# Rolling VectorE, ScalarE and the q projection of a one-token attention kernel, with wo loaded in five pieces

## The chip, the cores and the metric

The kernel runs on one core of a Trainium2 chip. The metric is the device time of one execution in microseconds (us). All runs that are compared here are in the fast state. Each kernel of the experiments was timed in five rounds beside the kernel before on the same chip; the experiments ran on three chips, on which the kernel before had medians of 662.74 (twice) and 662.91 us.

## The reference

One decode step of an attention block and a small feed-forward block, added up. Only the cache is large: K and V are 32 x 4 MB each.

```python
B, D, H, Sk, Dh, Dff = 2, 512, 32, 8192, 128, 1792      # one new token for each of 2 rows
xn = layernorm(x)
q = (xn @ wq) per head                                   # wq is 4 MB
p = softmax(q . k_cache * Dh**-0.5)                      # for each of the 64 (row, head) pairs
o = p . v_cache                                          # then o @ wo, wo is 4 MB
out = x + o @ wo + relu(xn @ w1) @ w2                    # w1, w2: 1792 KB each
```

## The kernel before: the parts that matter here

Two heads are one "pair", 4 MB of K and 4 MB of V. There are 32 pairs, two buffers for K and two for V. SyncE issues all large loads from one queue; wq borrows the second V buffer.

```python
nc.sync.dma_start(vs[1][:], wq).then_inc(dV[1], 16)
...
load_k(0); load_k(1); load_v(0)                  # SyncE
for t in range(NP - 1):
    if t + R < NP:
        sp.wait_ge(pT, NG * (t + 1))             # K buffer free: all transposes of pair t done
        load_k(t + R)
    sp.wait_ge(sW, t + 1)                        # V buffer free: weighted sum of pair t-1 done
    load_v(t + 1)
... x8, w1, w2, then wo in 3 pieces: cuts = (0, 16, 28, WJ) ...
```

TensorE projects q with 128 small matmuls written out one by one, and only then enters its loop over pairs:

```python
pe.wait_ge(dV[1], 16)                            # wq has landed
for h in range(H):
    for kt in range(KT):
        i = pe.matmul(qp[:, h, :], lhsT=wq_sb[:, kt, h*Dh:(h+1)*Dh], rhs=xnT[:, kt, :], ...)
i.then_inc(sQ, 1)
...
with pe.Fori(16, 16 * (NP // R) + 1, 16) as n16: # already rolled: two pairs a round
    for r in range(R):
        pe.reg_add(reg, reg, 1)
        step(r, reg, n16)                        # transposes of K, scores, weighted sum of the pair before
```

VectorE and ScalarE are written out over all 32 pairs in the kernel before (`for t in range(NP)`): they copy the transposed K from PSUM, find the maximum and do the exponential.

## Time and profile before

| | kernel before |
|---|---|
| time, median of 3 | 662.87 us (662.78 to 663.01) |
| span in the profile | 660.4 us |
| moved by DMA | 280.5 MB of data, mean 425 GB/s |
| TensorE, VectorE, ScalarE busy | 83%, 38%, 36% |
| q projection | 13.30 to 16.85 us |
| K0's transposes start / K2 issued | 24.27 / 36.53 us |
| last byte of wo / end of TensorE's wo matmuls | 655.75 / 656.82 us |

The page's lines for this kernel stand in the prediction below. A digit in the forty slices is a busy share in tenths. A row of stretches gives, from left to right, the stretch, its length, the busy time of TensorE's matmuls, its weight loads, VectorE, ScalarE and GpSimd with their counts, the granted clock, the DMA share and GB/s. The one thing to see is that the DMA engines are full from 3 us to 652 us (a DMA share of 0.99 to 1.00 in each stretch between), so the engines' busy shares decide nothing by themselves.

The 16 DMA engines can also be told apart. The records of packets carry no engine number, but from 60 to 600 us 16 packets are open in 95.6% of the time, and a 4 MB transfer is 128 packets of 32 KB, eight for each of 16. Strung together where one ends and the next starts, the packets give 16 chains, in which 98% of the gaps are under 30 ns. That a chain is an engine is an inference, and two chains that run in step can be taken for each other. How many engines still move data at a given time can be counted without chains, from the packets that are open then, and the groups below agree with that count.

### The profile page before, as it was taken

How to read it: one execution, taken by the hardware profiler on the slowest of the kernel's cores; microseconds unless marked ns; L12 is line 12 of the kernel's file. 1: busy time of each engine (PE TensorE's matmuls, PEld its weight loads, DVE VectorE, ACT ScalarE, POOL GpSimd, SP SyncE). 2: the span in 40 equal slices, each digit the busy share in tenths (PEclk: the TensorE clock that was granted, in tenths of full speed). 3: DMA queues.
4: the chain of work that ended last, by engine and by line, in shares of the span. 5: the costliest groups of instructions: out<-in, count | busy, mean ns of one | idle time of the engine just before them, and what ended most of it. 6: DMA issues, size and time to landing. Idle time of an engine off the chain costs nothing.

```text
span 660.4 us, 26876 instructions
## 1 busy us (share of the span) xinstructions
PE 551.0 (83%) x12864; PEld 537.0 (81%) x12864; DVE 251.4 (38%) x433; ACT 236.7 (36%) x389; POOL 8.5 (1%) x44
## 2 busy tenths in 40 slices
PE   2577999898887889788798987887997878987976
PEld 2577999888887889788798887887987878987875
DVE  1233544344343434434344443343443433443411
ACT  1242444343433334333243343333343333343410
POOL 1000000000000000000000000000000000000000
PEclk9999999998898999889899898899898989997985
DMA  9999999999999999999999999999999999999995
GB/s 381 416 438 429 424 439 427 437 427 431 437 429 437 427 431 433 429 437 429 431 435 427 439 429 431 435 427 439 427 431 433 429 439 425 435 433 429 437 417 246
DMA packets 10133, 280.73 MB, mean 425 GB/s; under 512 B 1154, under 2 KB 1156, under 8 KB 1284
## 3 DMA queue, kind: packets, MB, share of 16 engines
q1 hardware_dynamic: 10112, 280.50, 98.9%
q8 instruction: 10, 0.16, 0.1%
q14 instruction: 7, 0.06, 0.0%
q10 hardware_dynamic: 4, 0.00, 0.0%
HBM read 280.50 MB, written 0.00 MB: 425 GB/s over the span
## 4 chain that ended last, share of the span: by engine, by line
DMA 62%; PE 34%; ACT 1%; issue 1%; SPq 0%; DVE 0%
DMA ks<-in_A_k_cache_dram 56%; PE tp L233 21%; PE Sc L240 10%; DMA wo_sb<-in_A_wo_dram 5%; PE ot L253 3%; ACT kT L380 1%; PE ot L356 0%; PE Sc L288 0%; PE Sc L291 0%; SPq L171 0%; SPq L168 0%; SPq L166 0%; SPq L149 0%; SPq L167 0%; SPq L147 0%
## 5 line engine op out<-in xcount | busy, mean ns | idle before, releaser
L233 PE MATMUL tp<-identb,ks 128*128 128x128 bf16 x4096 | 324.9, 229 | 77.8 <-DMA ks<-in_A_k_cache_dram 75.9
L380 DVE COPY kT<-tp 128x1024 bf16<-128x1024 bf16 x320 | 219.7, 691 | 332.9 <-PE tp L233 332.7
L233 PEld LDWEIGHTS tp<-identb,ks 128*128 128x128 bf16 x4096 | 256.1, 103 | 81.3 <-DMA ks<-in_A_k_cache_dram 79.1
L380 ACT COPY kT<-tp 128x1024 bf16<-128x1024 bf16 x192 | 194.3, 1012 | 249.6 <-PE tp L233 249.6
L240 PE MATMUL Sc<-q,kT 128*128 128x64 bf16 x4096 | 216.3, 196 | 3.4 <-ACT kT L380 3.4
L240 PEld LDWEIGHTS Sc<-q,kT 128*128 128x128 bf16 x4096 | 178.4, 100 | 6.7 <-ACT kT L380 6.7
L253 PE MATMUL ot<-prm,vs 128*128 128x64 bf16 x4224 | 157.6, 193 | 8.5 <-issue 5.0
L253 PEld LDWEIGHTS ot<-prm,vs 128*128 128x128 bf16 x4224 | 140.5, 98 | 11.4 <-issue 8.8
L483 ACT COPY nm<-Sc 128x2 f32<-128x2 f32 x32 | 5.1, 160 | 118.2 <-PE Sc L291 118.2
L487 ACT ACTIVATE prm<-Sc,nm 64x128 bf16<-64x128 f32 x64 | 25.8, 402 | 1.4
L425 DVE TENSOR_REDUCE mcol<-Sc 64x1 bf16<-64x128 f32 x64 | 18.6, 291 | 17.6 <-PE Sc L240 17.2
L473 ACT COPY OTf<-ot 128x2 f32<-128x2 f32 x33 | 5.3, 160 | 35.3 <-PE ot L253 35.3
L430 DVE TENSOR_REDUCE mx<-Sc 1x2 bf16<-1x128 bf16 x32 | 8.9, 279 | 16.9 <-PE Sc L288 16.9
L203 POOL COPY q<-qb 128x2 bf16<-128x2 bf16 x32 | 5.8, 184 | 582.3 <-PE Sc L240 568.6
L487 ACT ACTIVATION_READ_ACCUMULATOR prm<-Sc,nm 64x1 f32 x64 | 11.8, 185 | 0.0
L218 PE MATMUL ot<-xnT,vs 128*128 128x2 bf16 x128 | 3.6, 165 | 8.3 <-DMA vs<-in_A_wq_dram 8.3
L218 PEld LDWEIGHTS ot<-xnT,vs 128*128 128x128 bf16 x128 | 3.5, 104 | 8.4 <-issue 8.4
L288 PE MATMUL Sc<-identb,mcol 128*1 128x128 bf16 x32 | 7.0, 217 | 0.0
L356 PE MATMUL ot<-OX,wo_sb 128*128 128x2 bf16 x128 | 3.7, 166 | 3.1 <-DMA wo_sb<-in_A_wo_dram 3.1
L356 PEld LDWEIGHTS ot<-OX,wo_sb 128*128 128x128 bf16 x128 | 3.6, 104 | 3.3 <-DMA wo_sb<-in_A_wo_dram 1.9
L291 PE MATMUL Sc<-mx,onesb 1*128 1x2 bf16 x32 | 5.5, 172 | 0.0
L436 DVE CAST xT<-tp 128x8 f32<-128x8 bf16 x1 | 0.2, 166 | 12.5 <-PE Sc L327 12.5
(49 smaller groups left out, 29.4 us busy)
## 6 DMA issues: line engine op xcount, KB each, us to landing
ks<-in_A_k_cache_dram SPq DMA_DIRECT2D x32, 4096.0 KB, 26.8
vs<-in_A_v_cache_dram SPq DMA_DIRECT2D x32, 4096.0 KB, 31.6
vs<-in_A_wq_dram SPq DMA_DIRECT2D x1, 4096.0 KB, 12.2
w_sb<-in_B_w_dram SPq DMA_DIRECT2D x2, 1792.0 KB, 25.9
wo_sb<-in_A_wo_dram SPq DMA_DIRECT2D x1, 2048.0 KB, 32.3
wo_sb<-in_A_wo_dram SPq DMA_DIRECT2D x1, 1536.0 KB, 35.5
wo_sb<-in_A_wo_dram SPq DMA_DIRECT2D x1, 512.0 KB, 36.3
xsb<-in_A_x_dram ACTq DMA_DIRECT2D x1, 2.0 KB
```

Source lines behind the costliest of these rows:

```text
L203: g.tensor_copy(q2[t % R][:], qb[:, 2 * t:2 * t + 2]).then_inc(sQ1, 1)
L218: i = pe.matmul(qp[:, h, :], lhsT=wq_sb[:, kt, h * Dh:(h + 1) * Dh], rhs=xnT[:, kt, :], start=(kt == 0), stop=(kt == KT - 1),)
L233: t = pe.transpose(tp[e % 4][:, i, :], ks[r][:, kk * Dh:(kk + 1) * Dh], identb[:])
L240: t = pe.matmul(Sc[r][:, 2 * kk:2 * kk + 2 * REP], lhsT=kT[e % 4][:, i, :], rhs=rep(q2[r][:]), start=True, stop=True,)
L253: t = pe.matmul(ot[r][:, 0:2 * REP], lhsT=vs[r][:, kk * Dh:(kk + 1) * Dh], rhs=rep(prm[r][:, kk, :]), start=(kk == 0), stop=(kk == KB - 1),)
L288: pe.transpose(tr_of(r), mcol[r][:], identb[:]).then_inc(sT, 1)
L291: pe.matmul(bc_of(r), lhsT=onesb[:], rhs=mx[r][:], start=True, stop=True).then_inc(sB, 1)
L356: t = pe.matmul(fin[:, c, :], lhsT=w[:, j, c * P:(c + 1) * P], rhs=act[:, j, :], start=(first and j == j0 and c == 0), stop=(last and j == ...
L380: fn(kT[e % 4][:], tp[e % 4][:]).then_inc(kR[e], 1)
L425: m = v.tensor_reduce(out=mcol[i][half, :], in_=S_of(i)[half, :, u], axis=AX.X, op=ALU.max)
L430: v.tensor_reduce(out=mx[i][:], in_=tr_of(i).rearrange("o (u m) -> o u m", u=2), axis=AX.X, op=ALU.max, negate=True,).then_inc(sX, 1)
L487: x = a.activation(out=prm[i][half, :, u], in_=S_of(i)[half, :, u], func=ACTF.Exp, bias=nm[i][half, u:u + 1], scale=1.0, accum_out=RS[half ...
```

## The change

The intent is less code and fewer instruction fetches: VectorE and ScalarE get loops as TensorE has one, the q projection becomes eight rounds of 16 matmuls, the engines' programs stand directly in the critical section, and wo comes in five pieces, so that fewer matmuls follow the last landing.

```diff
-    cuts = (0, 16, 28, WJ)
+    cuts = (0, 16, 22, 27, 30, WJ)
...
-    block = nc.Block(no_gpsimd_drain=True)
-    block.__enter__()
-    @block.sync
+    @(lambda f: f(nc.sync))                       # the same for the other four engines
...
-        for h in range(H):
-            for kt in range(KT):
-                i = pe.matmul(
-                    qp[:, h, :],
-                    lhsT=wq_sb[:, kt, h * Dh:(h + 1) * Dh],
+        HL = 4
+        with pe.Fori(0, H // HL) as hg:
+            for h in range(HL):
+                for kt in range(KT):
+                    i = pe.matmul(
+                        ot[1][:, bass.ds(hg * (HL * Bsz) + h * Bsz, Bsz)],
+                        lhsT=vs[1][:, bass.ds(hg * (HL * Dh) + (kt * H + h) * Dh, Dh)],
...
-        for t in range(NP):                       # VectorE; the same for ScalarE
-            i = t % R
+        def pair(i, n):
...
+        with v.Fori(0, NP // R):
+            for r in range(R):
+                v.reg_add(reg, reg, 1)
+                pair(r, reg)                      # waits count up to a register
```

(The semaphore of the transposes is split into one per group, so that the rolled engines can wait for a register's value; the diff is cut.)

More of the change, by code (lines that the diff above doesn't have):

```diff
@@ L121 @@
     dV = [sem(f"dV{i}") for i in range(R)]
-    dW = [sem(f"dW{i}") for i in range(5)]
+    dW = [sem(f"dW{i}") for i in range(2 + 5)]
     sG, sI, sQ, sQ1 = sem("sG"), sem("sI"), sem("sQ"), sem("sQ1")
     sV, sA, sE = sem("sV"), sem("sA"), sem("sE")
-    pT, sS, sT, sB, sW = sem("pT"), sem("sS"), sem("sT"), sem("sB"), sem("sW")
+    sS, sT, sB, sW = sem("sS"), sem("sT"), sem("sB"), sem("sW")
+    pT = [sem(f"pT{e}") for e in range(NG)]
     kR = [sem(f"kR{e}") for e in range(NG)]
-    sM, sX, sP, sO = sem("sM"), sem("sX"), sem("sP"), sem("sO")
+    sM, sX, sP, sO, sN = sem("sM"), sem("sX"), sem("sP"), sem("sO"), sem("sN")
     sH, sF = sem("sH"), sem("sF")
@@ L133 @@
     wo_v = A_wo.rearrange("(p j) n -> p j n", j=WJ)
-    cuts = (0, 16, 28, WJ)
+    cuts = (0, 16, 22, 27, 30, WJ)
+    NC = len(cuts) - 1
     qp = ot[1][:, 0:N].rearrange("p (h b) -> p h b", b=Bsz)
@@ L161, in _ @@
             if t + R < NP:
-                sp.wait_ge(pT, NG * (t + 1))
+                sp.wait_ge(pT[NG - 1], t + 1)
                 load_k(t + R)
@@ L168, in _ @@
         sp.dma_start(w2_sb[:], B_w2.rearrange("(p j) n -> p j n", j=FT)).then_inc(dW[1], 16)
-        for c in range(3):
+        for c in range(NC):
             sl = slice(cuts[c], cuts[c + 1])
@@ L175, in _ @@
         ).then_inc(dO, 16)
-    @block.gpsimd
+    @(lambda f: f(nc.gpsimd))
     def _(g):
@@ L203, in _ @@
             g.tensor_copy(q2[t % R][:], qb[:, 2 * t:2 * t + 2]).then_inc(sQ1, 1)
-    @block.tensor
+    @(lambda f: f(nc.tensor))
     def _(pe):
@@ L214, in _ @@
         pe.wait_ge(dV[1], 16)
-        wq_sb = vs[1][:].rearrange("p (kt n) -> p kt n", kt=KT)
-        for h in range(H):
-            for kt in range(KT):
-                i = pe.matmul(
-                    qp[:, h, :],
-                    lhsT=wq_sb[:, kt, h * Dh:(h + 1) * Dh],
-                    rhs=xnT[:, kt, :],
-                    start=(kt == 0),
-                    stop=(kt == KT - 1),
-                )
-        i.then_inc(sQ, 1)
+        HL = 4
[5 more added lines that the diff above has]
+                        lhsT=vs[1][:, bass.ds(hg * (HL * Dh) + (kt * H + h) * Dh, Dh)],
+                        rhs=xnT[:, kt, :],
+                        start=(kt == 0),
+                        stop=(kt == KT - 1),
+                    )
+            i.then_inc(sQ, 1)
         def rep(ap):
@@ L233, in transposes @@
                 t = pe.transpose(tp[e % 4][:, i, :], ks[r][:, kk * Dh:(kk + 1) * Dh], identb[:])
-            t.then_inc(pT, 1)
+            t.then_inc(pT[e], 1)
         def scores(r, e, n):
@@ L368, in _ @@
         pe.wait_ge(sV, 104)
-        for c in range(3):
+        for c in range(NC):
             pe.wait_ge(dW[2 + c], 16)
-            t = project(wo_sb, OX, cuts[c], cuts[c + 1], last=(c == 2))
+            t = project(wo_sb, OX, cuts[c], cuts[c + 1], last=(c == NC - 1))
         t.then_inc(sH, 1)
@@ L380, in kcopy @@
         fn(kT[e % 4][:], tp[e % 4][:]).then_inc(kR[e], 1)
-    @block.vector
+    @(lambda f: f(nc.vector))
     def _(v):
@@ L405, in _ @@
         v.tensor_copy(xnT[:], tpx).then_inc(sV, 1)
-        v.wait_ge(sQ, 2)
+        v.wait_ge(sQ, 1 + H // 4)
         v.tensor_scalar(
@@ L414, in _ @@
         ).then_inc(sV, 94)
-        for t in range(NP):
-            i = t % R
+        def pair(i, n):
             for e in range(NG):
                 if e not in ON_ACT:
-                    v.wait_ge(pT, NG * t + e + 1)
+                    v.wait_ge(pT[e], n)
                     kcopy(v, e)
-            v.wait_ge(sS, t + 1)
+            v.wait_ge(sS, n)
             for u in range(2):
@@ L428, in _ @@
             m.then_inc(sM, 1)
-            v.wait_ge(sT, t + 1)
+            v.wait_ge(sT, n)
             v.tensor_reduce(
@@ L433, in _ @@
             ).then_inc(sX, 1)
+        reg = nc.alloc_register(mybir.EngineType.DVE, "pairno_v")
+        v.reg_mov(reg, 0)
+        with v.Fori(0, NP // R):
+            for r in range(R):
+                v.reg_add(reg, reg, 1)
+                pair(r, reg)
         v.wait_ge(sH, 1)
@@ L439, in _ @@
         v.tensor_tensor(
-            out=OTn[:].rearrange("p b h -> p (b h)"), in0=OTf[:, 0:N], in1=RD[:], op=ALU.mult
+            out=OTn[:].rearrange("p b h -> p (b h)"), in0=OTf[:, 2:N + 2], in1=RD[:], op=ALU.mult
         ).then_inc(sV, 1)
@@ L460, in _ @@
         v.tensor_copy(osb[:], tp[1][0:Bsz * KT, 0, :]).then_inc(sE, 1)
-    @block.scalar
+    @(lambda f: f(nc.scalar))
     def _(a):
@@ L468, in _, with out_copy, pair @@
         ).then_inc(sA, 1)
-        def out_copy(t):
-            c = 2 * t if t >= 0 else N
-            a.wait_ge(sW, t + 2)
-            a.copy(OTf[:, c:c + 2], ot[t % R][:, 0:2]).then_inc(sO, 1)
-        a.copy(OTf[:, N:N + 1], eps_t[:]).then_inc(sO, 1)
-        for t in range(NP):
-            i = t % R
+        def out_copy(r, n, c):
+            a.wait_ge(sW, n)
+            a.copy(OTf[:, bass.ds(c, 2)], ot[r][:, 0:2]).then_inc(sO, 1)
+        def pair(i, n, t):
             for e in range(NG):
                 if e in ON_ACT:
-                    a.wait_ge(pT, NG * t + e + 1)
+                    a.wait_ge(pT[e], n)
                     kcopy(a, e)
-            a.wait_ge(sB, t + 1)
-            a.copy(nm[i][:], bc_of(i)).then_inc(sA, 1)
-            a.wait_ge(sA, t + 2)
+            a.wait_ge(sB, n)
+            a.copy(nm[i][:], bc_of(i)).then_inc(sN, 1)
+            a.wait_ge(sN, n)
             for u in range(2):
@@ L492, in _ @@
                     scale=1.0,
-                    accum_out=RS[half, t:t + 1],
+                    accum_out=RS[half, bass.ds(t, 1)],
                 )
             x.then_inc(sP, 1)
-            out_copy(t - 1)
-        out_copy(NP - 1)
-    block.__exit__(None, None, None)
+            out_copy(1 - i, n, t * 2)
+        a.copy(nm[0][:, 0:1], eps_t[:]).then_inc(sO, 1)
+        reg = nc.alloc_register(mybir.EngineType.Activation, "pairno_a")
+        a.reg_mov(reg, 0)
+        with a.Fori(0, NP // R) as tr:
+            for r in range(R):
+                a.reg_add(reg, reg, 1)
+                pair(r, reg, tr * R + r)
+        out_copy(1, NP + 1, N)
     nc.sync.wait_ge(dO, 16)
```

## The prediction

> **What bounds the kernel now.** I read the page's forty slices first, then the stretches, then the DMA issues in order of time, then the two ends.
>
> ```profile
> span 660.4 us, 26876 instructions
> DMA  9999999999999999999999999999999999999995
> q1 hardware_dynamic: 10112, 280.50, 98.9%
> q8 instruction: 10, 0.16, 0.1%
> q14 instruction: 7, 0.06, 0.0%
> ```
> ```profile
> 0.00:37.00 37.00, 16.52 (x386) 16.40 (x387) 8.96 (x19) 7.73 (x9) 3.00 (x14) 1.00 0.96 407
> 37.00:107.00 70.00, 62.31 (x1522) 60.41 (x1519) 29.70 (x52) 30.31 (x49) 0.74 (x4) 1.00 1.00 428
> 107.00:620.00 513.00, 441.94 (x10226) 431.13 (x10223) 203.77 (x345) 192.22 (x320) 4.79 (x26) 0.94 1.00 432
> 652.00:660.40 8.40, 3.26 (x108) 2.91 (x105) 0.38 (x2) 0.00 (x0) 0.00 (x0) 0.50 0.21 81
> ```
> The last two columns of a stretch are the DMA share and GB/s. The DMA engines are full from about 3 us to 652 us at 432 GB/s; 280.5 MB at 432 GB/s is 649 us of the 660. The 83% of TensorE is not the bound: a pair of heads takes it 15.9 us (K issues at 75.81 and 91.66 below), while 8.39 MB of K and V take 19.4 us. So time is won or lost only where the DMA engines run dry, where something else uses them, or after their last byte.
>
> How near to dry they come, from the SyncE issues (L144 is K, L147 is V):
> ```profile
> 1.40 0.90 SPq L144 DMA_DIRECT2D ks<-in_A_k_cache_dram  x2
> 2.34 0.53 SPq L147 DMA_DIRECT2D vs<-in_A_v_cache_dram  x1
> 36.53 0.33 SPq L144 DMA_DIRECT2D ks<-in_A_k_cache_dram  x1
> 44.48 0.33 SPq L147 DMA_DIRECT2D vs<-in_A_v_cache_dram  x1
> 57.41 0.33 SPq L144 DMA_DIRECT2D ks<-in_A_k_cache_dram  x1
> 75.81 0.33 SPq L144 DMA_DIRECT2D ks<-in_A_k_cache_dram  x1
> 91.66 0.33 SPq L144 DMA_DIRECT2D ks<-in_A_k_cache_dram  x1
> ```
> A packet of 32 KB takes a DMA engine 1.213 us in the packet records, and a 4 MB transfer is eight on each engine: 9.7 us. Four transfers (wq, K0, K1, V0) are queued at the start, so with data flowing from about 2.9 us they end at 41.7 us. K2 is issued at 36.53 and needs about 1.2 us to start (wq: issued at 0.96, packets from 2.0 to 3.1). **Slack at the head: about 4 us.** Later landings take 26.8 us from issue, nearly three transfers, so there the slack is far larger.
>
> The q projection is what precedes all that on TensorE:
> ```profile
> 13.30 3.55 PE L218 MATMUL ot<-xnT,vs 128*128 128x2 bf16 x128 [8.33 <-DMA vs<-in_A_wq_dram]
> 16.96 0.22 DVE L408 TENSOR_SCALAR qb<-ot 128x64 bf16<-128x64 f32 x1 [11.80 <-PE ot L218]
> 24.27 2.74 PE L233 MATMUL tp<-identb,ks 128*128 128x128 bf16 x24 [7.43 <-DMA ks<-in_A_k_cache_dram]
> ```
> It takes 3.55 us (27.7 ns a matmul), and TensorE then idles 7.4 us for K0.
>
> The tail:
> ```profile
> 654.96 1.86 PE L356 MATMUL ot<-OX,wo_sb 128*128 128x2 bf16 x64 [1.83 <-DMA wo_sb<-in_A_wo_dram]
> 656.87 0.17 DVE L453 TENSOR_TENSOR yT<-ot,xT 128x8 bf16<-128x8 f32 x1 [8.25 <-PE ot L356]
> ```
> wo pieces 2 and 3 land at 654.9 and 656.2, and 64 matmuls follow the earlier landing. Following the packets engine by engine (each packet starts where the last one of its engine ended), the 16 DMA engines do not finish together: six at 652.2 to 652.8 us, eight at 653.9 to 654.4, two at 655.6 and 655.75. The laggards are those that also carried **instruction fetches**: a 16 KB fetch (TensorE; nine before the end) puts its engine about 1.5 us back, an 8 KB one (VectorE, ScalarE; three each) 0.6 to 1 us. One of the last two engines carried three 8 KB fetches, the other two 16 KB ones, at 68.4 and 652.0 us.
>
> [...] this trace has 208 ns in the median:
> ```profile
> L297 PEldq FUSED_REGOPS  x16: 35/35/35, 16.4 to 595.1; - x16
> L297 PEldq ALU_OP  x16: 32/32/32, 64.3 to 633.6; - x16
> L297 PEldq COMPARE_BRANCH  x16: 76/208/244, 64.4 to 633.7; - x16
> ```
> [...]
>
> **The change, part by part.**
>
> 1. *Rolled q projection.* The built program has eight rounds of 16 matmuls with a fused register instruction before each matmul, whose addresses come from registers. Sequencer instructions follow each other here at about 93 ns (a fused one at 64.678, the next at 64.771 us), not at their 35 ns. So 128 x (93 + 28) = 15.5 us, plus 8 x about 0.35 us for the counter and branch (64.375 to 64.678 us is 0.30) = 18.3 us; reading two register addresses per matmul may add to it. If the sequencer overlaps the two it is nearer 14. I take 18 to 21 us against 3.55. Q is then ready at 13.3 + Q + about 0.7 us, K0's transposes start there instead of at 24.27, and K2's issue follows 12.3 us later as before. The DMA engines run dry for 13.3 + Q + 0.7 + 12.3 + 1.2 - 41.7 = **Q - 14.2 us**: 0 at 14, 4 at 18, 7 at 21, 16 at 30. K3 and later issues should add nothing: TensorE gains 3.5 us a pair[...].
>
> 2. *Rolled VectorE and ScalarE.* Their programs fall from 450 and 342 instructions to 63 and 51, so their six 8 KB fetches vanish and the engine with three of them leaves the last place. Against it: register waits, three fused instructions a pair on ScalarE (0.3 us), a branch per two pairs, and a table load which the build places inside ScalarE's loop: 16 x 1.28 = 20 us of ScalarE time. All that lies beside 3.5 us of TensorE slack a pair: 0.
>
> 3. *TensorE's code* shrinks by 204 instructions (matmuls counted twice)[...], so I expect eight fetches before the end instead of nine. The only engine hit twice was hit by fetches seven and nine. If eight land on eight engines, the last finishes at about 654.3: **-1.4 us**; if two still meet, 0.
>
> 4. *wo in five pieces.* After the last landing 8 matmuls remain: 0.23 us. Before, the end at 656.82 was 0.6 us after the landing at 656.2: -0.35 us. Sixteen more packets an engine at 8.5 ns fixed cost (12 KB take 460 ns, 4 KB 159) give back 0.14: **-0.2 us**.
>
> 5. *No inner block.* wq is issued before it anyway; at the end its barrier is over at 658.44, before the output lands (658.88): 0.
>
> Sum: +4 to +7 for the head, -0.2 to -1.6 for the tail: 665 to 669. I weigh in a third of a chance that the rolled loop costs less and hides, and settle at +3.2 us: 666.0.
>
> **The rivals.** (a) *All of it is hidden, and only fetches and tail count*: 661 to 662. For it: 7.4 us idle plus 4 us of slack. Against it: the 93 ns spacing. (b) *The head bounds*: the q projection is paced by the sequencer and DMA runs dry near 42 us: 665 to 670, up to 678 if register addresses cost 100 ns a matmul more. (c) *ScalarE becomes the bound through table loads and register work*: it is 36% busy, the load adds 3%; only in the first 100 us could 1 us a round matter. I give it 5%. (d) *Fetch collisions stay*: the tail gain drops to 0.2 us.
>
> **Range and chances.** The measured 662.87 is 2.5 us above the span; I keep that. The low end is (a) with the full tail gain, 661; the high end is Q of about 27 us, 674. Faster by over 2% would need 13 us off a span with 649 us of transfers: 1%. Slower by over 2% needs Q above 28 us: 6%.
>
> **What would show it.** Step 1: the q projection's matmuls spread over 18 us or more, K0's transposes starting after 30 us, K2's issue after 43 us, and a slice near 42 to 48 us with a low DMA share. If Q ends before 27 us, or the share stays full, step 1 is wrong. Step 2: no 8 KB fetches between 0 and 650 us, a table load in each round, the middle at 432 GB/s. Step 3: the last wo landing 1.5 us nearer to the bulk of the packets' end. Step 4: 8 matmuls after the last landing. The prediction fails upwards if register-addressed matmuls are far slower than a sequencer step, or if ScalarE's loop holds TensorE up early; it fails downwards if the sequencer runs ahead of the array.

The 208 ns are the median of a compare-and-branch in the trace of before, whose two table loads took 1283 ns each. That 204 instructions fewer save a fetch was the estimate; the profiles show nine 16 KB packets on q8 for the changed kernel and ten before.

## The result

The changed kernel takes **669.27 us** (median of 6, 668.58 to 669.92), the kernel before on the same chip 662.88 (662.78 to 663.06): 6.4 us longer. The ratio is 1.0096, with a 95% interval of 1.0083 to 1.0109. Ratios here are the mean time of one kernel's fast runs over that of the other's of the same rounds, so not quite the ratio of the medians. The interval is clear of 1. The point forecast was 666.0: the direction and the place of the loss were right, the size was half.

From the page of the changed kernel:

```profile
span 667.6 us, 27260 instructions
DMA  9959999999999999999999999999999999999996
GB/s 377 438 224 406 438 436 432 424 436 436 432 422 438 436 432 422 438 436 432 422 438 436 432 420 440 434 432 422 440 432 430 426 440 432 430 426 440 432 415 264
q8 instruction: 9, 0.15, 0.1%
q14 instruction: 1, 0.01, 0.0%
```

The third slice, 33 to 50 us, has half the DMA share of its neighbours. The six 8 KB fetches of the body are gone from q14. The stretches of the changed kernel, cut at the edges of the gap:

```profile
0.00:41.80 41.80, 24.42 (x219) 20.14 (x220) 4.35 (x12) 5.38 (x7) 3.01 (x14) 1.00 0.95 401
41.80:49.30 7.50, 7.50 (x188) 7.50 (x186) 4.84 (x7) 3.63 (x4) 0.00 (x0) 1.00 0.07 17
49.30:107.00 57.70, 53.00 (x1281) 51.42 (x1278) 23.89 (x42) 24.25 (x42) 0.74 (x4) 0.97 1.00 428
107.00:620.00 513.00, 446.38 (x10368) 435.56 (x10366) 208.55 (x351) 214.00 (x333) 4.80 (x26) 0.95 1.00 432
```

For 7.5 us the DMA engines move next to nothing, while TensorE is busy without a break: it is late, and they wait for it. From 107 to 620 us the rate is 432 GB/s as before, so nothing is lost in the body. What TensorE did until then, in order of time:

```profile
13.72 2.19 PE L219 MATMUL ot<-xnT,vs 128*128 128x2 bf16 x16 [9.11 <-DMA vs<-in_A_wq_dram]
16.40 2.20 PE L219 MATMUL ot<-xnT,vs 128*128 128x2 bf16 x16 [0.48 <-issue]
...
32.18 2.20 PE L219 MATMUL ot<-xnT,vs 128*128 128x2 bf16 x16 [0.43 <-issue]
34.49 0.22 DVE L409 TENSOR_SCALAR qb<-ot 128x64 bf16<-128x64 f32 x1 [29.68 <-PE ot L219]
...
35.19 2.72 PE L234 MATMUL tp<-identb,ks 128*128 128x128 bf16 x24 [0.82 <-POOL q L203]
```

A round of 16 matmuls takes 2.63 us from start to start, the projection 20.7 us (13.72 to about 34.4) against 3.55. K0's transposes wait for q now, 35.19 instead of 24.27. The view of the line itself shows why (durations in ns, least, median and most):

```profile
L219 PE MATMUL ot<-xnT,vs x128: 163/183/185, 13.7 to 34.2; 128*128 128x2 bf16 x128
L219 PEldq FUSED_REGOPS  x120: 46/46/79, 13.7 to 34.1; - x120
```

Before nearly every matmul TensorE's sequencer works out an address in a fused register instruction. In the trace's records one such instruction starts 124 ns after the one before it where the first takes 46 ns, and 158 ns where it takes 79 ns. They go in turn with the matmuls: the weight load starts 96 ns after a register instruction of 46 ns, the matmul 6 ns later, the next register instruction 22 ns after that. Between two rounds the sequencer counts and branches (line 216):

```profile
L216 PEldq COMPARE_BRANCH  x8: 76/208/223, 15.9 to 34.3; - x8
```

From the last matmul of a round to the first of the next it is mostly 613 ns, so the seven seams hold about 3.5 us more than seven ordinary steps of 124 ns. SyncE's issues then follow:

```profile
48.31 0.33 SPq L146 DMA_DIRECT2D ks<-in_A_k_cache_dram  x1
53.43 0.33 SPq L149 DMA_DIRECT2D vs<-in_A_v_cache_dram  x1
65.48 0.33 SPq L146 DMA_DIRECT2D ks<-in_A_k_cache_dram  x1
```

K2 is issued at 48.31 us, 13.1 us after the transposes began, and 6.5 us after the four transfers at the start had ended. The table loads in ScalarE's loop are there as forecast (16 of 1283 ns) and cost nothing that shows. In the tail the last wo piece leaves 8 matmuls:

```profile
663.26 0.37 PE L357 MATMUL ot<-OX,wo_sb 128*128 128x2 bf16 x8 [0.15 <-DMA wo_sb<-in_A_wo_dram]
663.67 0.17 DVE L460 TENSOR_TENSOR yT<-ot,xT 128x8 bf16<-128x8 f32 x1 [9.58 <-PE ot L357]
```

The chains of packets show the rest. "Last byte" is the end of the last packet of wo.

| DMA engines by the end of their data | before | changed |
|---|---|---|
| not set back by a fetch | six, 652.2 to 652.8 | ten, 660.7 to 661.3 |
| set back once | eight, 653.9 to 654.4 | six, 662.3 to 662.8 |
| set back twice, or by three 8 KB fetches | two, 655.6 and 655.75 | none |
| last byte | 655.75 | 662.77 |

The undisturbed engines end 8.4 us later, the last byte only 7.0 later. So the head costs 8.4 us, and 1.4 us come back because no engine is set back twice. Counted packet by packet, as a mean of the 16 engines, the changed kernel's DMA engines stand idle for 7.8 us between 5 and 600 us (0.1 in the kernel before), and the first packets after the gap, which take up to 2.0 us instead of 1.2, cost another 0.6. TensorE's nine fetches before the end also add up: two (at 41.9 and 46.1 us) fall into the dry stretch, one (at 660.97) starts when its engine's data has ended, and the other six are one for each of the six engines set back.

### The profile page after: what moved, and what is told of

It reads as the page before. It is cut to its first block, busy times and chain, and to the rows that moved or that the text cites. A ratio compares the mean times of both kernels' runs of the same rounds, so it can differ in the third digit from the quotient of the medians.

```text
span 667.6 us, 27260 instructions
## 1 busy us (share of the span) xinstructions
PE 566.4 (85%) x12864; PEld 548.3 (82%) x12864; DVE 251.3 (38%) x433; ACT 256.0 (38%) x404; POOL 8.5 (1%) x44
## 4 chain that ended last, share of the span: by engine, by line
DMA 56%; PE 39%; ACT 2%; issue 2%; SPq 0%; DVE 0%; ACTq 0%; POOL 0%; DVEq 0%; POOLq 0%
DMA ks<-in_A_k_cache_dram 48%; PE tp L234 21%; PE Sc L241 11%; DMA wo_sb<-in_A_wo_dram 6%; PE ot L254 5%; PE ot L219 3%; DMA vs<-in_A_wq_dram 2%; ACT kT L381 2%; ACT L381 1%; SPq L171 0%; PE Sc L289 0%; PE Sc L292 0%; SPq L168 0%; PE ot L357 0%; SPq L166 0%
## 5 line engine op out<-in xcount | busy, mean ns | idle before, releaser
L219 PE MATMUL ot<-xnT,vs 128*128 128x2 bf16 x128 | 17.6, 182 | 12.2 <-DMA vs<-in_A_wq_dram 9.1
L219 PEld LDWEIGHTS ot<-xnT,vs 128*128 x128 | 13.3, 104 | 16.4 <-issue 12.6
L381 ACT ACT_TABLE_LOAD x16 | 20.5, 1283 | 2.2
L480 ACT COPY OTf<-ot 128x2 f32 (+1 forms) x33 | 5.3, 160 | 28.3 <-PE ot L254 28.3
L492 ACT ACTIVATION_READ_ACCUMULATOR prm<-Sc,nm x64 | 11.8, 184 | 0.0
```

The source lines that it names most:

```text
L219: i = pe.matmul(ot[1][:, bass.ds(hg * (HL * Bsz) + h * Bsz, Bsz)], lhsT=vs[1][:, bass.ds(hg * (HL * Dh) + (kt * H + h) * Dh, Dh)], rhs=xnT ...
L381: fn(kT[e % 4][:], tp[e % 4][:]).then_inc(kR[e], 1)
L480: a.copy(OTf[:, bass.ds(c, 2)], ot[r][:, 0:2]).then_inc(sO, 1)
L492: x = a.activation(out=prm[i][half, :, u], in_=S_of(i)[half, :, u], func=ACTF.Exp, bias=nm[i][half, u:u + 1], scale=1.0, accum_out=RS[half ...
```

## The experiments

**Theory A**: register-computed addresses pace the q projection; K2 is issued too late and the DMA queue runs dry once; the cost is a threshold and then a us for each us. **Theory B**: rolled VectorE and ScalarE, with their register waits and table loads, cost the time. **Theory C**: every part costs a little.

| run | this, us | before, us | ratio (95% interval) | last byte, us |
|---|---|---|---|---|
| e1, q written out | 662.61 | 662.74 | 0.9998 (0.9984 to 1.0012) | 655.80 |
| e2, only q rolled | 670.52 | 662.74 | 1.0113 (1.0098 to 1.0129) | 663.93 |
| e3, 16 of 32 heads rolled | 664.08 | 662.74 | 1.0014 (1.0000 to 1.0027) | 656.47 |
| e4, 24 of 32 heads rolled | 665.02 | 662.74 | 1.0032 (1.0018 to 1.0046) | 658.37 |
| e5, q rolled, w1 early | 666.84 | 662.74 | 1.0060 (1.0046 to 1.0074) | 657.40 |
| e6, rolled, fixed addresses (wrong result) | 661.38 | 662.74 | 0.9979 (0.9965 to 0.9992) | 654.42 |
| e7, only VectorE and ScalarE rolled | 663.19 | 662.74 | 1.0006 (0.9992 to 1.0020) | 655.67 |
| e8, only five pieces | 662.62 | 662.74 | 0.9998 (0.9984 to 1.0012) | 655.73 |
| e9, half rolled, w1 early | 663.33 | 662.91 | 1.0007 (0.9993 to 1.0021) | 656.14 |
| e10, q written out, w1 early | 663.45 | 662.91 | 1.0011 (0.9998 to 1.0025) | 655.90 |

Times are medians of five runs (four for e2); the last byte is from the profiled run. For e5 that is the fastest of its five, 665.65 us, 1.2 below the median.

### e1 and e2: the q projection alone

```diff
 e1, against the changed kernel                    e2, against the kernel before
-        with pe.Fori(0, H // HL) as hg:           -        for h in range(H):
+        for h in range(H):                        +        with pe.Fori(0, H // HL) as hg:
```

> The changed kernel with the q projection written out again, all else kept. Theory A (the rolled q projection takes 20.7 us, K2 is issued too late and the DMA engines run dry once for about 7.7 us, plus some 0.7 us of restart): the dry stretch goes, the time is 669.3 minus 8 to 8.5, 660.8 to 661.3 us, or up to 662.4 if TensorE's nine instruction fetches hit one DMA engine twice again; DMA share full in all slices from 5 us on. Theory B (rolled VectorE and ScalarE, their register waits and the 16 table loads cost the time): 666 us or more. Theory C (all parts cost a little): 664 to 666.

> The kernel before with only the q projection rolled. Theory A: before plus 8 to 8.5, so 670.5 to 671.5 us; the engine with three 8 KB fetches still ends last. Theory B: 663 to 664. Theory C: 664 to 667.

e1 is the changed kernel without its rolled q: 662.61 us, 6.7 us below it, and equal to the kernel before. e2 is the kernel before with the rolled q alone: 7.8 us above it, as forecast. Theory B is out: in e1 the rolled VectorE and ScalarE, the table loads and the register waits are all there, and nothing is lost. The expected 660.8 to 661.3 did not come, though; what came is 0.2 us above the upper end of the expectation, 662.4 with two fetches on one engine. In e1 eight engines end at 652.4 to 652.7, seven at 654.1 to 654.6 and one at 655.80: TensorE's code has its full length again (ten packets on q8, nine in the changed kernel), nine of its fetches come before their engine's data has ended (eight in e6 below), they set seven engines back once and one twice, and the tail gain is lost.

### e6: a rolled loop with fixed addresses

All eight rounds compute the first four heads (VectorE clears the PSUM columns first). Its output is wrong, which doesn't matter for the time.

```diff
-    ot[1][:, bass.ds(hg * (HL * Bsz) + h * Bsz, Bsz)],
-    lhsT=vs[1][:, bass.ds(hg * (HL * Dh) + (kt * H + h) * Dh, Dh)],
+    ot[1][:, h * Bsz:(h + 1) * Bsz],
+    lhsT=vs[1][:, (kt * H + h) * Dh:(kt * H + h + 1) * Dh],
```

> WRONG RESULT ON PURPOSE: q rolled in the same eight rounds of 16 matmuls, but with fixed addresses (every round computes the first four heads), so that the fused register instructions before the matmuls are gone. Theory A (the register instructions pace the loop): a round takes 16 x 28 ns plus 0.3 to 0.4 us, q about 6.5 us, no dry stretch, and TensorE's code stays a block shorter, so the fetches need not meet on one DMA engine: 661.0 to 661.5 us if they do not, 662.6 if they do. A rival by which the branch and loop, not the addresses, cost the time: q over 13 us and 665 us or more.

"A block" is here what one 16 KB fetch brings.

Its line of the projection in order of time, and its first K issue that waits:

```profile
13.46 3.73 PE L219 MATMUL ot<-xnT,vs 128*128 128x2 bf16 x128 [8.84 <-DMA vs<-in_A_wq_dram]
```
```profile
35.15 0.33 SPq L146 DMA_DIRECT2D ks<-in_A_k_cache_dram  x1
```

All 128 matmuls run in one piece in 3.73 us (about 6.5 were expected), though the branches are as long as in the changed kernel:

```profile
L216 PEldq COMPARE_BRANCH  x8: 76/208/223, 13.6 to 16.8; - x8
```

The first branch is taken at 13.64 us, while the matmuls of its round start until 13.86: the sequencer runs ahead of the array. So a loop without computed addresses costs 0.2 us here. With the register instructions the sequencer is no longer ahead, and both they and the seams show: of the 17 us, about 3.5 lie in the seams and the rest between the matmuls of a round. Without the address instructions both go. The time is 661.38 us, the fastest of all. TensorE's code stays one 16 KB fetch shorter (nine packets on q8, ten in e1): eight engines end at 652.4 to 653.0, none after 654.4. Against e1, which differs in nothing else that shows, the last byte comes 1.4 us earlier and the time is 1.2 us shorter. This is what the change would have brought if rolling q had been free.

### e3 and e4: how much of q is rolled

```diff
-        with pe.Fori(0, H // HL) as hg:
+        with pe.Fori(0, 4) as hg:                 # e4: 6; the other heads written out behind the loop
```

> The changed kernel with 16 of the 32 heads of q rolled and 16 written out: q takes about 4 x 2.63 + 4 x 0.44 = 12.3 us. Theory A says the cost is a threshold, q time minus about 13 us: nothing is left, the same time as with q written out within 0.4 us (nearly 661). A rival by which each us of q costs a us says half of the cost is left: 665 us.

> The changed kernel with 24 of 32 heads of q rolled: q takes about 6 x 2.63 + 2 x 0.44 = 16.7 us. Theory A (a threshold near 13 us of q time, then a us for a us): the DMA engines run dry for about 3.6 us from 41.8 us on, against 7.6 with all rolled: 666 to 667 us. A rival by which any rolling costs a fixed amount: 664 (as with half) or 669 (as with all).

The third column is the end of the undisturbed DMA engines against e6's.

| rolled heads | q takes | K2 issued | undisturbed engines later by | time |
|---|---|---|---|---|
| none written in addresses (e6) | 3.7 us | 35.15 | 0 | 661.38 |
| 16 (e3) | 12.1 us | 39.64 | 1.3 us | 664.08 |
| 24 (e4) | 16.5 us | 43.98 | 4.2 us | 665.02 |
| 32 (changed) | 20.7 us | 48.31 | 8.4 us | 669.27 |

```profile
39.64 0.33 SPq L146 DMA_DIRECT2D ks<-in_A_k_cache_dram  x1
```
```profile
43.98 0.33 SPq L146 DMA_DIRECT2D ks<-in_A_k_cache_dram  x1
```

The first line is e3's, the second e4's. Up to a little under 40 us K2's issue is free; from there each us of lateness is nearly a us of the end: 4.3 us later from e4 to the changed kernel, 4.2 us later at the end. A fixed cost of rolling is out, and so is a us for each us of q from the start. e3 was expected at e1's time within 0.4 us and came out 1.5 us above it: it stands at the edge. Counted packet by packet, its DMA engines are idle for only about 0.2 us more than e6's, near 42 and 61 us, but packets between 40 and 44 us and between 58 and 64 us, where the next K is issued close to its limit too, take 0.8 us longer in all; the two make 1.0 of the 1.3 us. Its times also spread most, 662.68 to 664.79. e4 came out 1 us below the expected range, though its dry time came as forecast (3.4 us idle by the packets, 3.6 expected): the range fits e1's 662.6 as its base, with two fetches on one engine, while e4 has e6's short code and no engine set back twice. On e6's 661.38 its 4.2 us give 665.6.

### e5: fill the dry stretch with something else

```diff
         load_v(0)
+        sp.dma_start(w1_sb[:], B_w1...).then_inc(dW[0], 16)    # was behind the last V
```

> The changed kernel, q still rolled, with the load of w1 (1.79 MB, about 4.2 us of all DMA engines) moved from the end to the start of the queue, behind V0. Theory A: it fills 4.2 of the 7.7 us of dry time, and the end has 4.2 us less to load: 665.0 to 665.6 us, K2 issued as late as before. A rival by which TensorE's lateness itself, not the dry DMA queue, sets the end says no change: 669.3.

The stretches of e5 around the place of the gap, and its K2:

```profile
41.80:46.00 4.20, 4.20 (x101) 4.20 (x98) 2.56 (x4) 2.27 (x3) 0.00 (x0) 1.00 0.92 383
46.00:48.20 2.20, 2.20 (x66) 2.20 (x64) 1.38 (x2) 0.76 (x1) 0.00 (x0) 1.00 0.31 88
```
```profile
47.13 0.33 SPq L146 DMA_DIRECT2D ks<-in_A_k_cache_dram  x1
```

K0's transposes start hardly earlier (35.06 us) and K2 is issued 1.2 us earlier: a round of eight transposes and eight score matmuls takes 0.69 us from 38.87 us on, in the changed kernel from 41.44 on, after rounds of 1.28; why is open. The last byte comes 5.4 us earlier than in the changed kernel: 4.2 us of w1, and 1.2 us of K2. So it is the dry queue and not TensorE's lateness that sets the end. The median falls by 2.4 us only, to 666.84, above the expected 665.0 to 665.6. The profiled run took 665.65, 3.9 less than that of the changed kernel (669.57); what the other four lost beyond it no trace shows. In the profiled run 1.5 of the 5.4 us are missing, and they are in the tail:

```profile
657.69 2.02 PE L357 MATMUL ot<-OX,wo_sb 128*128 128x2 bf16 x70 [1.77 <-issue]
```

V31 lands 14.2 us before the last byte and no longer 18.5, which leaves TensorE less time, and before the last 70 of its wo matmuls, in the middle of the first piece, it stands still for 1.8 us, waiting for no data. An instruction fetch runs from 655.1 to 656.2 us, and TensorE goes on 1.5 us after its end. Six waits early in the kernel before and in the changed one, between 40 and 77 us, end 1.3 to 1.5 us after a 16 KB fetch in the same way. That the fetch is the cause is likely, and not shown by a run of its own.

### e7 and e8: the other parts alone

e7 keeps the rolled VectorE and ScalarE and takes everything else back; e8 is the kernel before with the five cuts.

```diff
 e8, against the kernel before
-    cuts = (0, 16, 28, WJ)
+    cuts = (0, 16, 22, 27, 30, WJ)
```

> The kernel before with VectorE and ScalarE rolled, nothing else. Theory A: their six fetches vanish, but the last DMA engine is still the one that TensorE's fetches hit twice, 655.6 us: 662.7 us, no change within 0.3. Rival: the rolled engines' register waits and table loads cost time: 664 or more.

> The kernel before with wo in five pieces, nothing else. Theory A: 8 instead of 16 matmuls behind the last landing and no wait of them behind the third piece, less the cost of 16 more packets per DMA engine: 662.4 to 662.7 us. Rival: smaller packets and more issues cost more than they bring: 663 or more.

Neither changes the time beyond its interval. In e7 the six 8 KB fetches are gone, and the last byte still comes at 655.67 us, because by the chains two of TensorE's fetches meet on one engine as before. In e8 the last byte comes at 655.73; any gain of the shorter end is within the noise. Removing the inner block was not run alone; e1 and e7 differ in it and in the pieces, and by 0.6 us, less than the spread of e7 (662.64 to 663.80).

### e9 and e10: is there a version that beats both?

> Half of the heads rolled (as in the run with 16 rolled heads, 664.1 us) and w1 loaded behind V0. Theory A (that run lost about 1.3 us to short dry spells of the DMA queue between 42 and 64 us): w1 in the queue removes them, and TensorE's code is 76 instructions shorter than with q written out, so the fetches may miss each other: 661.5 to 662.8 us; up to 664 if TensorE waits for an instruction fetch in the tail, as it did for 1.8 us in the run with w1 early and all of q rolled. It is a try at a version that beats both.

> Control: q written out and w1 loaded behind V0. Theory A: the DMA queue was never dry with q written out, so early w1 brings nothing: 662.3 to 663.5 us, slower only if V31, landing 4 us later, makes TensorE late at the end. A rival by which early w1 is worth something by itself says 660 us or less.

Both use e5's edit, e9 on e3, e10 on e1. Neither beats the kernel before: 663.33 and 663.45 us. e10, the control, came out as expected: early w1 brings nothing where the queue is never dry (663.45 us, 662.91 before). e9 missed its 661.5 to 662.8, inside the reserve up to 664. In its trace e3's dry spells and slow packets are gone; but the 0.8 us between the two medians are not clear of noise, as their intervals overlap. No correct kernel here is faster than the one before; the 1.4 us of e6 would need shorter TensorE code without computed addresses.

## Why the prediction was right or wrong

- **The bound** was right: the body runs at 432 GB/s in both kernels, and time was lost at the head and won at the end of the queue.
- **Step 1, duration of the projection**: forecast 18 to 21 us, measured 20.7. The spacing read from the trace of before carried over: 124 ns for the shorter fused instruction and its matmul, against 93 + 28. One fused instruction in five is longer (158 ns), and a seam takes 0.49 us more than an ordinary step, where 0.35 were put.
- **Step 1, dry time**: the formula "Q - 14.2 us" gives 6.5 for the measured Q, and the undisturbed engines ended 8.4 us later. Three terms were short: the projection began at 13.72 and not 13.30 us (0.4), K2's issue came 13.1 us after the first transposes and not 12.3 (0.8), and the restart of the queue, which had no term beyond the 1.2 us to start, cost another 0.6 to 0.7.
- **Step 2** was right (e1, e7): the fetches vanish, the table loads and register waits hide.
- **Step 3** was right: no engine is set back twice in the changed kernel, and e6 against e1 gives 1.4 us of last byte. The count was a bit different in the changed kernel itself: of its eight fetches before the end of its data, two fell into the dry time and so set no engine back.
- **Step 4 and step 5**: 0.2 us and 0 were forecast; e8 shows no more than the noise for the pieces, and the inner block was not run alone.
- **The step that failed** is the last one: "I weigh in a third of a chance that the rolled loop costs less and hides, and settle at +3.2 us: 666.0". The sum itself stood at 665 to 669 (its ends give 665.3 and 669.7); with the measured Q and the full tail gain its own terms give 662.9 + 6.5 - 1.6 = 667.8. The weighted-in case, a sequencer that overlaps register work with matmuls, did not come: in e6 it runs ahead over branches, but in the changed kernel register instruction, weight load and matmul start in turn, 124 ns a step, and the projection takes 20.7 us. Of the 3.3 us missing from 666.0, 1.8 are this averaging; the other 1.5 are the head's short terms (1.9 us in the trace, whose run was 0.3 us above the median).

With the measured terms the books close: e6's 661.38, plus 8.4 us at the head, is 669.8 against 669.27 measured.

## What to carry to other kernels

Before rolling a loop, ask what its addresses depend on: here the branches were hidden while the addresses were fixed, and with computed addresses the projection took about 134 ns more for each matmul of 28 ns ((20.7 - 3.55) us over 128), a fifth of it in the seams between rounds. Look also for a deadline of the work ahead of the first freed buffer (bytes queued over the rate). In this kernel, bound by DMA at 432 GB/s, the four transfers of 4 MB queued at the start ended at 41.8 us: with K2 issued at 35.15 us (e6) the work was free, and from 43.98 (e4) to 48.31 us (the changed kernel) 4.3 us of lateness cost 4.2 us at the end. And a mean of two outcomes that exclude each other is a poor forecast: the sum of the terms was nearer than the hedge.
